# W' of three batches by Strassen's method in blocks, with the scores of later batches closer together

## The chip, the cores and the metric

The program runs on one core of a Trainium2 chip. The metric is the device time of one execution in microseconds (us), as a median of three runs. Of the core's engines, TensorE (PE in the profile) multiplies, VectorE (DVE) and ScalarE (ACT) do elementwise work, and SyncE (SP) issues the DMA transfers. Each engine works through its own list in order and waits where an operand or a buffer is not ready.

## The reference

```
B, N, C = 4, 6080, 256          d_model = 256, d_ff = 2048
qn = q / (norm(q, axis=1) + 1e-6);  kn = k / (norm(k, axis=1) + 1e-6)
a  = softmax(kn^T @ qn / tau, last axis) with + 1e-9 in the divisor     # 256 x 256 for each batch
x  = (v @ a) as 24320 rows of 256
out = max(0.01 h, h) @ w_out,  h = x @ w_in                            # float32 throughout
```

## The kernel before, in words

The kernel never forms x. Since h = v (a w_in), it makes W' = a w_in (256 x 2048) once for each batch and multiplies v by it. All products are in float32 precision from fp32r halves: each operand is split into a high and a low part, and three passes (high x high, low x high, high x low) are added up in PSUM.

**Tiles and steps.** The rows of v are taken in 24 tiles, six for each batch: five of 2 x 512 columns and one of 2 x 480. Each tile i is worked through in NPAIR = 8 steps p, each with one pair of blocks of W'; this text counts steps as s = 8 i + p, from 0 to 191, 48 for each batch. A step multiplies v by W' with Strassen's method in Winograd's form, seven products of three matmuls: A11 and A12 first, then S2, S1, S3, A22 and S4 (`block_product`), into the PSUM banks x and z. Between them ScalarE copies h11, h12 and h22 out of bank x (`taken`), VectorE adds bank z to them (`add`), and `leaky` applies the activation and splits the result. The step's 24 matmuls with w_out (`ffn_out`, L675) are issued during the next step by `out(n)`, in blocks of 5, 5, 8 and the remaining 6. So a step has 21 + 24 = 45 matmuls.

**Work beside it.** What the next batch needs is made during the current one: the scores k^T q of the 48 chunks (`chunk_work`: `cast` on ScalarE, `low` on VectorE, four matmuls `product`, and the squares for the norms), the norms and the softmax (`norm_work`, `row_work`), the transpose (`turn_work`) and then W' (`w_work`). The scores of batches 0 and 1 are made at the start of the program. W_in, split into halves, lies in DRAM as `win_dram` in blocks of 512 columns. A W' product (`w_product`, L463) has 6 matmuls: three passes over the two halves of the inner dimension; there are two for each of NWC = 4 column blocks j. Its copy goes to `w_parts`, which makes the sums of the blocks and splits them in six pieces: two sums (0.8 each), then `begin` (1.0) and `rest` (1.2) for each of two p. Every `begin` and `rest` takes a buffer of the tag qk_split (three buffers) and stores it to `w_dram`. The score casts use the same tag. `w_load` fetches the split blocks three steps ahead.

**The order.** The order on TensorE, VectorE and ScalarE is that of the program text: `in_order` ties each instruction to the one before it on its engine. DMA issues are not tied in that way. The work beside stands in queues `todo`, with a length for each entry that is a planner's figure; `slot(queue, room)` takes entries from the head as long as they fit. An entry may put others when it is issued, at the head where `first` is set. This text names the slots of a step (i > 0) in their order in the program:

- after A11 and A12: A1 (act, 0.65), the addition to h11, D1 (dve, 1.3), `out(5)`, P1 (pe, room 1)
- `leaky` of C11, D2 (dve, 2.2), block S2, the copy of h12, A2 (act, 1.8), block S1, `out(5)`, P2 (pe, 1)
- block S3, the copy of h22 and the addition to it, D3 (dve, 1.3), `out(8)`, P3 (pe_late, 1)
- `leaky` of C22, blocks A22 and S4, the addition to h12, `leaky` of C21, A3 (act, 0.65), D4 (dve, 0.8), `leaky` of C12, `out(24)`

The feed-forward work on v for the next tile (`v_work`) also stands in the dve queue. Work for batch b starts at `w0` = 48 (b - 1); `at(w, ...)` puts it at step w. Before, the norms come at step e, the rows at e + 2, the transpose at e + 4 and W' from e + 5 on.

Of the kernel before, what the change touches and what calls it, by code (L numbers as in the profile page):

```python
# [17 lines left out]
P = 128  # L18
TW = 512
# [5 lines left out]
WARM = 5  # L25
VBUFS = 10
# [6 lines left out]
def channel_attention_ffn(  # L33
# [44 lines left out]
    def temp(dtype=F32, name="temp"):  # L78
        return work.tile([P, TW], dtype, name=name, tag="temp", bufs=10)
# [34 lines left out]


    class Scores:
# [133 lines left out]
        def norms_begun(self):  # L250
# [84 lines left out]
        def turned_high(self):  # L335
            self.aT = small.tile([P, 2, CH, C], F32R, name="aT")
            return nc.scalar.copy(out=self.aT[:, 0], in_=self.t_ps)

        def turned_low(self):
            return nc.vector.tensor_tensor(  # L340
                out=self.aT[:, 1], in0=self.t_ps, in1=f32(self.aT[:, 0]), op=ALU.subtract
            )

# [93 lines left out]
    def win_load(j):  # L437
        for h in range(CH):
            win[j, h] = win_tile(False)
            nc.sync.dma_start(out=flat(win[j, h]), in_=win_dram[j][h])  # L440


# [25 lines left out]
    def w_tmp(name):  # L468
        return work.tile([P, TW], F32, name=name, tag="w_tmp", bufs=4)
# [81 lines left out]
    def w_load(i, p):  # L551
        w = w_tile()
# [107 lines left out]
    def ffn_out(i, p):  # L660
# [8 lines left out]
        for name, f, j in (("C11", f1, 0), ("C22", f2, 1), ("C21", f2, 0), ("C12", f1, 1)):  # L669
# [13 lines left out]
            if p == NPAIR - 1 and not early:  # L683
# [5 lines left out]
                for h, a, z, copy, queue in parts:  # L689
                    o = work.tile([P, TW], F32, name="o_sb", bufs=4)  # L690
# [21 lines left out]
    def put(queue, length, fn, then=(), first=False):  # L712
# [10 lines left out]

        (todo[queue].appendleft if first else todo[queue].append)((length, run))
# [8 lines left out]

    def chunk_work(sc, j):

        put("act", 0.6, lambda: sc.cast(j), [
            ("dve", 0.75, lambda: sc.low(j), [("pe_next", 1, lambda: sc.product(j))]),
        ])
# [400 lines left out]
```

## Time and profile before

| what | value |
|---|---|
| median of three runs | 2163.67 us (2163.30 to 2164.05) |
| the profiled execution | 2164.93 us, of which its span 2163.1 us |
| TensorE, matmuls | 2155.5 us busy, 9674 instructions |
| TensorE, weight loads | 1797.3 us busy |
| VectorE | 1464.7 us busy, 2602 instructions |
| ScalarE | 1468.1 us busy, 2545 instructions |
| DMA | 337.15 MB, 155 GB/s of HBM traffic over the span |

The span runs from the first to the last instruction. Matmuls overlap each other, so their busy time is that in which at least one runs. A share of busy time is an average over the whole span; what a change is worth is read from the place where it is made and from what waits there.

### The profile page before, as it was taken

The numbers are of one execution on the slowest core, as the hardware profiler recorded it, in microseconds if no ns is written. First come the engines' busy times: TensorE is split into PE (matmuls) and PEld (weight loads), VectorE is DVE, ScalarE is ACT, GpSimd is POOL, SyncE is SP. The second block draws the span as 40 slices with busy tenths as digits, with TensorE's granted clock in tenths as the row PEclk, the third lists the DMA queues.
The fourth block names the chain that finished last, engine by engine and source line by source line (L and its number), as shares of the span: only waits on it lengthen the run. The fifth ranks groups of instructions, "written<-read, shape, count | busy, mean of one in ns | idle before, by whom it ended". The sixth has DMA issues, their size and how long they took to land.

```text
span 2163.1 us, 26727 instructions
## 1 busy us (share of the span) xinstructions
PE 2155.5 (100%) x9674; PEld 1797.3 (83%) x9674; DVE 1464.7 (68%) x2602; ACT 1468.1 (68%) x2545; POOL 3.3 (0%) x11
## 2 busy tenths in 40 slices
PE   9999999999999999999999999999999999999999
PEld 8888888888888888888888888888888888888887
DVE  7987667657767666776776767666667555555554
ACT  6577777766677777776667777777656666666665
POOL 0000000000000000000000000000000000000000
PEclk9999999999999999999999999999999999999999
DMA  9945445435544343442654434344264332332331
GB/s 345 391 174 184 161 147 189 158 109 197 197 169 153 125 147 114 163 161 86 216 175 171 150 122 155 131 138 153 88 229 173 114 131 105 109 137 104 106 121 35
DMA packets 106179, 337.15 MB, mean 156 GB/s; under 512 B 11072, under 2 KB 23360, under 8 KB 106048
## 3 DMA queue, kind: packets, MB, share of 16 engines
q1 hardware_dynamic: 105680, 335.14, 44.9%
q8 instruction: 76, 1.25, 0.2%
q14 instruction: 55, 0.45, 0.1%
q10 hardware_dynamic: 368, 0.32, 0.1%
HBM read 276.96 MB, written 58.46 MB: 155 GB/s over the span
## 4 chain that ended last, share of the span: by engine, by line
PE 97%; DMA 1%; DVE 1%; ACT 0%; issue 0%; SPq 0%; ACTq 0%; DVEq 0%
PE ps_o L675 48%; PE ps_x L628 24%; PE ps_z L628 18%; PE ps_s L193 3%; PE ps_s L463 2%; PE ps_y L193 2%; PE ps_o L193 1%; DMA qk_raw<-in_k_dram 1%; PE ps_y L463 0%; PE ps_y L628 0%; DVE v_split L593 0%; SPq L141 0%; PE ps_z L463 0%; DVE h L649 0%; DVE g_split L642 0%
## 5 line engine op out<-in xcount | busy, mean ns | idle before, releaser
L675 PE MATMUL ps_o<-g_split,w_out_split 128*128 128x512 f32 (+1 forms) x4608 | 1161.6, 387 | 0.0
L675 PEld LDWEIGHTS ps_o<-g_split,w_out_split 128*128 128x128 f32 x4608 | 864.7, 188 | 173.9
L642 DVE TENSOR_TENSOR g_split<-h,g_split 128x512 fp32r<-128x512 f32 (+1 forms) x768 | 524.8, 684 | 387.7 <-ACT g_split L640 386.9
L628 PE MATMUL ps_x<-v_split,w_split 128*128 128x512 f32 (+1 forms) x2304 | 647.6, 389 | 0.0
L649 DVE TENSOR_TENSOR h<-ps_z,h 128x512 f32<-128x512 f32 (+1 forms) x568 | 387.4, 682 | 269.1 <-ACT h L655 263.7
L639 ACT ACTIVATE h<-h 128x512 f32<-128x512 f32 (+1 forms) x576 | 361.9, 628 | 263.1 <-DVE h L649 263.1
L655 ACT COPY h<-ps_x 128x512 f32<-128x512 f32 (+1 forms) x576 | 334.3, 580 | 297.5 <-PE ps_x L628 297.0
L628 PEld LDWEIGHTS ps_x<-v_split,w_split 128*128 128x128 f32 x2304 | 424.7, 188 | 80.3 <-ACT h L655 1.3
L640 ACT CAST g_split<-h 128x512 fp32r<-128x512 f32 (+1 forms) x768 | 473.6, 617 | 24.2
L628 PE MATMUL ps_z<-v_split,w_split 128*128 128x512 f32 (+1 forms) x1704 | 477.0, 388 | 0.3 <-DVE h L649 0.3
L628 PEld LDWEIGHTS ps_z<-v_split,w_split 128*128 128x128 f32 x1704 | 319.0, 188 | 66.8 <-DVE h L649 2.5
L639 ACT ACTIVATE h<-ps_x 128x512 f32<-128x512 f32 (+1 forms) x192 | 112.8, 588 | 11.6 <-PE ps_x L628 11.4
L593 DVE TENSOR_TENSOR v_split<-v_raw,v_split 128x512 fp32r<-128x512 f32 (+1 forms) x144 | 98.6, 686 | 5.8 <-DMA f_raw<-in_w_out_dram 0.6
L163 DVE TENSOR_TENSOR sq_acc<-sq_acc,sq 128x512 f32<-128x512 f32 x141 | 96.1, 682 | 0.0
L160 ACT ACTIVATE sq<-qk_raw 128x512 f32<-128x512 f32 x141 | 89.4, 634 | 0.0
L168 ACT CAST qk_split<-qk_raw 128x512 fp32r<-128x512 f32 x96 | 59.4, 619 | 25.5 <-PE ps_y L193 21.7
L172 DVE TENSOR_TENSOR qk_split<-qk_raw,qk_split 128x512 fp32r<-128x512 f32 x96 | 65.6, 683 | 2.3 <-ACT qk_split L168 2.3
L193 PE MATMUL ps_s<-qk_split 128*128 128x512 f32 x192 | 64.0, 333 | 0.0
L193 PE MATMUL ps_y<-qk_split 128*128 128x512 f32 x192 | 59.8, 336 | 0.0
L589 DVE CAST v_split<-v_raw 128x512 fp32r<-128x512 f32 (+1 forms) x138 | 57.3, 415 | 0.0
L193 PE MATMUL ps_s<-qk_raw 128*128 128x256 f32 x192 | 44.1, 381 | 1.8 <-DMA qk_raw<-in_k_dram 1.8
L193 PE MATMUL ps_o<-qk_raw 128*128 128x256 f32 x192 | 43.5, 390 | 0.4 <-DMA qk_raw<-in_k_dram 0.4
(113 smaller groups left out, 731.6 us busy)
## 6 DMA issues: line engine op xcount, KB each, us to landing
w_split<-w_dram SPq DMA_DIRECT2D x184, 896.0 KB, 4.7
qk_raw<-in_q_dram SPq DMA_DIRECT2D x115, 256.0 KB, 3.6
qk_raw<-in_k_dram SPq DMA_DIRECT2D x115, 256.0 KB, 4.1
v_raw<-in_vT_dram SPq DMA_DIRECT2D x40, 512.0 KB, 5.5
out_dram<-o_sb SPq DMA_DIRECT2D x80, 256.0 KB, 3.7
win<-win_dram SPq DMA_DIRECT2D x24, 512.0 KB, 3.9
w_dram<-w_rest SPq DMA_DIRECT2D x24, 512.0 KB, 3.1
w_dram<-w_first SPq DMA_DIRECT2D x24, 384.0 KB, 3.0
```

The lines of the kernel that those rows point to most:

```text
L160: return nc.scalar.activation(out=out, in_=self.chunk(j), func=AF.Square)
L163: return nc.vector.tensor_tensor(out=self.acc[0], in0=self.acc[0], in1=sq, op=ALU.add)
L172: return nc.vector.tensor_tensor(out=sp[:, :, 1, :], in0=self.chunk(j), in1=f32(sp[:, :, 0, :]), op=ALU.subtract)
L193: mm = nc.tensor.matmul(out=out, lhsT=lhsT, rhs=rhs, start=start, stop=stop, skip_group_check=True)
L593: last = nc.vector.tensor_tensor(out=sp[:, 1, 0:w], in0=src, in1=f32(sp[:, 0, 0:w]), op=ALU.subtract)
L628: mm = nc.tensor.matmul(out=ps[:, 0:n], lhsT=w[:, x, a, :], rhs=sp[:, y, 0:n], start=first and k == 0, stop=k == 2, skip_group_check=True,)
L639: nc.scalar.activation(out=out[:, 0:n], in_=h[:, 0:n], func=AF.Prelu, alpha=0.01)
L640: issued["act"] = nc.scalar.copy(out=sp[:, 0, 0:n], in_=out[:, 0:n])
L642: issued["dve"] = nc.vector.tensor_tensor(out=sp[:, 1, 0:n], in0=out[:, 0:n], in1=f32(sp[:, 0, 0:n]), op=ALU.subtract)
L649: issued["dve"] = nc.vector.tensor_tensor(out=h[:, 0:n], in0=ps[:, 0:n], in1=h[:, 0:n], op=ALU.add)
L655: issued["act"] = nc.scalar.copy(out=h[:, 0:n], in_=ps[:, 0:n])
L675: issued["pe"] = nc.tensor.matmul(out=o_ps[i][j][h][:, 0:n], lhsT=wo[x][:, f, h * P:(h + 1) * P], rhs=sp[:, y, 0:n], start=p == 0 and earl ...
```

## The change

W' of batches 1 to 3 is multiplied in blocks. With the four 128 x 128 blocks of a and the 128 x 512 blocks of W_in, two neighbouring column blocks (a pair q) take seven products of three matmuls, where they took four of six. `w_pair` issues them one after another: the first four add up in one PSUM bank and are copied by ScalarE after each, the last three are added by VectorE to those copies. After the seventh, `split(0)` and `split(1)` put the twelve pieces of `w_parts`, and the second pair follows. The sums of the W_in blocks are made once, at steps 10 and 20 (`sums_work`), and kept in DRAM as `win_sums`. The sums of the blocks of a and their halves are made after the transpose (`blocks_taken` to `blocks_low`). Of batch 0, W' stays as it was.

The chain from the norms to W' is now put as one list in which each entry follows when the one before it has been issued (`put_steps`), and cut finer: `norms_begun` has one Newton step, `norms_went` two; `maxima` is apart from `scaled`. The scores of batches 2 and 3 start at offset 0 of their 48 steps and take 28 instead of 31; the squares of batch 1 take 20 steps instead of 25. A cast waits in its queue while three are ahead of their products, and P1 takes up to three entries when at least two wait. Buffers: `temp` has 12 and serves `o_sb` too (before 10, and 4 of its own), `w_tmp` 6 instead of 4.

```
     def temp(dtype=F32, name="temp"):
-        return work.tile([P, TW], dtype, name=name, tag="temp", bufs=10)
+        return work.tile([P, TW], dtype, name=name, tag="temp", bufs=TEMPS)
...
             self.nt = small.tile([P, n], F32, name="nt")
-            return self.newton(x, self.ny, self.nt, 2)
+            return self.newton(x, self.ny, self.nt, 1)
+
+        def norms_went(self):
+            return self.newton(self.nx, self.ny, self.nt, 2)
 
         def norms(self):
             x, y, t, n = self.nx, self.ny, self.nt, 2 * CH
-            self.newton(x, y, t, 1)
...
-                nc.vector.scalar_tensor_tensor(
+                last = nc.vector.scalar_tensor_tensor(
                     out=s[:, h, :], in0=self.sum_of(h), scalar=self.rk[:, h:h + 1], in1=self.rq,
                     op0=ALU.mult, op1=ALU.mult,
                 )
+            self.e = s
+            return last
+
+        def maxima(self):
             self.nm = small.tile([P, CH], F32, name="nm")
-            self.e = s
-            return nc.vector.tensor_reduce(out=self.nm, in_=s, axis=AX.X, op=ALU.max, negate=True)
+            return nc.vector.tensor_reduce(out=self.nm, in_=self.e, axis=AX.X, op=ALU.max, negate=True)
...
     def w_tmp(name):
-        return work.tile([P, TW], F32, name=name, tag="w_tmp", bufs=4)
 
     def w_load(i, p):
+        assert (i // NT, p) in w_done
...
                 for h, a, z, copy, queue in parts:
-                    o = work.tile([P, TW], F32, name="o_sb", bufs=4)
+                    o = work.tile([P, TW], F32, name="o_sb", tag="temp", bufs=TEMPS)
                     copy(out=o[:, a:z], in_=o_ps[i][j][h][:, a:z])
                     queue.dma_start(out=outT[h * P:(h + 1) * P, n0 + a:n0 + z], in_=o[:, a:z])
...
-        while todo[queue] and todo[queue][0][0] <= room:
+        while todo[queue] and todo[queue][0][0] <= room and todo[queue][0][1].ready():
...
-        ])
+        def cast():
+            cast_ahead.append(j)
+            return sc.cast(j)
+
+        def product():
+            cast_ahead.pop(0)
+            return sc.product(j)
+
+        put("act", 0.6, cast, [("dve", 0.75, lambda: sc.low(j), [("pe_next", 1, product)])],
+            ready=lambda: len(cast_ahead) < 3)
...
     def norm_work(sc):
-        norms = ("pe_late", 1, sc.norms_mm, [
-            ("dve", 0.5, sc.norms_taken, [("dve", 1.8, sc.norms_begun, [("dve", 2.0, sc.norms)], True)], True),
-        ])
-        if len(sc.s) == 1:
-            put(*norms)
-        else:
-            put("act", 0.8, sc.cross_taken, [("dve", 0.9, sc.cross_added), norms])
-
-    def row_work(sc):
-        put("pe_late", 1, sc.rows_mm, [
-            ("dve", 0.5, sc.rows_taken, [
-                ("dve", 1.8, sc.scaled, [("act", 0.6, sc.exps, [("dve", 1.1, sc.normed, (), True)], True)], True),
-            ], True),
-        ])
+        norms = [("pe_late", 1, sc.norms_mm), ("dve", 0.4, sc.norms_taken), ("dve", 0.9, sc.norms_begun),
+                 ("dve", 1.2, sc.norms_went), ("dve", 1.2, sc.norms), ("pe_late", 1, sc.rows_mm),
+                 ("dve", 0.5, sc.rows_taken), ("dve", 1.0, sc.scaled), ("dve", 0.7, sc.maxima),
+                 ("act", 1.3, sc.exps), ("dve", 1.1, sc.normed), ("call", turn_work, sc)]
+        if len(sc.s) > 1:
+            norms[:0] = [("act", 0.8, sc.cross_taken), ("dve", 0.9, sc.cross_added)]
+        put_steps(norms, False)
 
     def turn_work(sc):
-        put("pe", 1, sc.turn, [("act", 0.6, sc.turned_high, [("dve", 0.7, sc.turned_low, (), True)], True)])
-
-    def w_work(b, j, h=0):
-
-
-        def taken():
-            ins = w_taken(b, j, h)
-            if h == 0:
-                w_work(b, j, 1)
+        put_steps([("pe", 1, sc.turn), ("act", 0.65, sc.blocks_taken), ("dve", 0.9, sc.blocks_summed),
+                   ("act", 1.3, sc.blocks_high), ("dve", 1.3, sc.blocks_low), ("call", w_pair, sc.b, 0)], False)
...
+    def sums_work(q):
+
+        blocks = {(h, x): win_in(win_dram[2 * q + x][h]) for h, x in ((0, 1), (0, 0))}
+        t = {}
...
+        def halves(name, x):
+            def high():
+                t[name, 0] = work.tile([P, 2, TW], F32R, name="win_t", tag="qk_split", bufs=3)
+                return nc.scalar.copy(out=t[name, 0][:, 0, :], in_=t[name])
+
+            def low():
+                r = t[name, 0]
+                ins = nc.vector.tensor_tensor(out=r[:, 1, :], in0=t[name], in1=f32(r[:, 0, :]), op=ALU.subtract)
+                nc.sync.dma_start(out=win_sums[q][x], in_=flat(r))
+                return ins
+            return [("act", 0.65, high), ("dve", 0.7, low)]
+
+        def more():
+            for h, x in ((1, 1), (1, 0)):
+                blocks[h, x] = win_in(win_dram[2 * q + x][h])
+
+        put_steps([
+            whole("a", 0, 1), whole("b", 0, 0), minus("b", "a", "b"), *halves("b", 0),
+            ("call", more),
+            whole("c", 1, 1), minus("a", "c", "a"), *halves("a", 2), minus("c", "c", "b"), *halves("c", 1),
+            whole("d", 1, 0), minus("d", "d", "c"), *halves("d", 3),
+        ], False)
+
+    A_S1, A_S2, A_S3, A_S4, A_11, A_12, A_22 = range(7)
+
+    def w_pair(b, q):
+
+        operands = [win_dram[2 * q][0], win_sums[q][1], win_sums[q][2], win_sums[q][3],
+                    win_sums[q][0], win_dram[2 * q + 1][1], win_dram[2 * q][1]]
+        of = (A_11, A_S2, A_S3, A_22, A_S1, A_S4, A_12)
+        loaded, c = {}, {}
+
+        def load(n):
+            if n < 7:
+                loaded[n] = win_in(operands[n])
+
+        def product(n):
+            m, r = scores[b].m, loaded.pop(n)
+            if n in (0, 4, 6):
+                c["ps"] = bank("s")
+            for k, (x, y) in enumerate(PASSES):
+                last = nc.tensor.matmul(
+                    out=c["ps"], lhsT=m[:, x, of[n], :], rhs=r[:, y, :], start=n in (0, 4, 6) and k == 0, stop=k == 2,
+                    skip_group_check=True,
+                )
+            load(n + 2)
+            return last
+
+        def taken(n):
+            if n == 0:
+                for name in ("c11", "c21", "c12", "c22"):
+                    c[name] = w_tmp("w_a")
+            out = c[("c11", "c12", "c22", "c21", "c22", "c12", "c11")[n]]
+            if n < 4:
+                return nc.scalar.copy(out=out, in_=c["ps"])
+            return nc.vector.tensor_tensor(out=out, in0=out, in1=c["ps"], op=ALU.add)
+
+        def split(x):
+            j = 2 * q + x
+            for h in range(CH):
+                a_sb[b, j, h] = c[("c11", "c21", "c12", "c22")[2 * x + h]]
+            for length, fn in w_parts(b, j):
+                put("dve", length, fn)
+            length, fn = todo["dve"].pop()
+            if x == 0:
+                put("dve", length, fn, [("call", split, 1)])
+            elif q + 1 < NWC // 2:
+                put("dve", length, fn, [("call", w_pair, b, q + 1)])
             else:
-                for length, fn in w_parts(b, j):
-                    put("dve", length, fn)
-                if j + 1 < NWC:
-                    length, fn = todo["dve"].pop()
-                    put("dve", length, fn, [("call", w_work, b, j + 1)])
-            return ins
-
-        if h == 0 and j + 1 < NWC:
-            win_load(j + 1)
-        put("pe", 1, lambda: w_product(b, j, h, "s"), [("act", 0.6, taken, (), True)])
+                todo["dve"].append((length, fn))
+
+        def step(n):
+            after = [("call", step, n + 1)] if n < 6 else [("call", split, 0)]
+            put("pe", 1, lambda: product(n), [
+                ("act" if n < 4 else "dve", 0.65, lambda: taken(n), after, True)
+            ])
+
+        load(0)
+        load(1)
+        step(0)
...
     for b in range(1, B):
         w0 = (b - 1) * WPB
         sc = scores[b]
-        begin_at, span = (NPAIR, 25) if b == 1 else (2, 31)
+        begin_at, span = (NPAIR, 20) if b == 1 else (0, 28)
         when = {j: w0 + begin_at + j * span // NCHUNK for j in range(NCHUNK)}
         for i in range(len(sc.groups)):
-            at(max(w0, when[i * G] - 3), lambda sc=sc, i=i: sc.load(i, qk_raw()))
+            at(max(w0 - 2, when[i * G] - (1 if b == 1 else 3)), lambda sc=sc, i=i: sc.load(i, qk_raw()))
         for j in range(NCHUNK):
             at(when[j], square_work if b == 1 else chunk_work, sc, j)
         e = w0 + begin_at + span + 1
         at(e, norm_work, sc)
-        at(e + 2, row_work, sc)
-        at(e + 4, turn_work, sc)
-        at(e + 1, win_load, 0)
-        at(e + 5, w_work, b, 0)
+    for pair in range(NWC // 2):
+        at(10 + 10 * pair, sums_work, pair)
...
             out(5)
-            slot("pe", 1 if i else 2)
+            slot("pe", 1 if i and len(todo["pe"]) < 2 else 3)
```

## Rows read from the trace of the kernel before

**Rows 1.** The profile page of the kernel before: busy time of TensorE (PE) and of its weight loads (PEld) with their shares of the span and their instructions, and TensorE's granted clock in 40 slices, in tenths of full speed.

```profile
PE 2155.5 (100%) x9674; PEld 1797.3 (83%) x9674; DVE 1464.7 (68%) x2602; ACT 1468.1 (68%) x2545; POOL 3.3 (0%) x11
...
PEclk9999999999999999999999999999999999999999
```

**Rows 2.** The page's chain of work that ended last: shares of the span by engine.

```profile
PE 97%; DMA 1%; DVE 1%; ACT 0%; issue 0%; SPq 0%; ACTq 0%; DVEq 0%
```

**Rows 3.** The same chain in order of time: start in us, length in us, engine, tile, line and count of the merged piece. Each row is the third output block of a step (8 matmuls of L675), of which every step has one: steps 9 and 10, which hold no other matmuls, two neighbours in the scores of batch 2, and two neighbours in the stretch in which W' of batch 2 is made.

```profile
197.62 1.81 PE ps_o L675 x8
...
207.82 1.81 PE ps_o L675 x8
...
637.35 1.82 PE ps_o L675 x8
...
648.97 1.82 PE ps_o L675 x8
...
1029.56 1.81 PE ps_o L675 x8
...
1042.48 1.81 PE ps_o L675 x8
```

**Rows 4.** Busy time in a stretch of ten steps of tile 2 and 3 (batch 1 squares running beside the feed-forward work): from, to, length, then busy us and instructions of PE, PEld, VectorE (DVE), ScalarE (ACT) and GpSimd, the granted clock, the DMA share and GB/s.

```profile
306.00:408.00 102.00, 102.00 (x451) 84.46 (x450) 71.96 (x116) 75.69 (x131) 0.00 (x0) 1.00 0.46 158
```

**Rows 5.** The instructions of L463, the W' products, in bank s (batches 1 to 3): shortest, median and longest duration in ns, first and last start, form.

```profile
L463 PEld LDWEIGHTS ps_s<-win,aT x144: 187/188/188, 502.2 to 1642.5; 128*128 128x128 f32 x144
L463 PE MATMUL ps_s<-win,aT x144: 387/393/398, 502.5 to 1642.7; 128*128 128x512 f32 x144
```

**Rows 6.** TensorE's instructions in order of time (start us, length us, engine, line, operation, output<-inputs, shape, count): around the norms and the exps of batch 2, the second W' product of step 87, and the A22 block of step 96.

```profile
986.21 1.98 PE L675 MATMUL ps_o<-g_split,w_out_split 128*128 128x512 f32 x8
988.20 1.02 PE L229 MATMUL ps_s<-ones,sq_acc 128*128 128x1 f32 x8
...
1007.79 1.98 PE L675 MATMUL ps_o<-g_split,w_out_split 128*128 128x512 f32 x8
1009.62 0.61 PE L284 MATMUL ps_y<-diag,ones 128*128 128x128 f32 x4
...
1018.47 1.98 PE L675 MATMUL ps_o<-g_split,w_out_split 128*128 128x512 f32 x8
1020.33 0.96 PE L628 MATMUL ps_x<-v_split,w_split 128*128 128x512 f32 x3
1021.13 0.87 PE L628 MATMUL ps_z<-v_split,w_split 128*128 128x512 f32 x3
...
1040.28 1.52 PE L463 MATMUL ps_s<-win,aT 128*128 128x512 f32 x6
...
1140.84 0.84 PE L628 MATMUL ps_x<-v_split,w_split 128*128 128x512 f32 x3
```

**Rows 7.** ScalarE's instructions in order of time, same columns; in brackets the idle time before one and what ended it. The copy of h22 behind the exps, the copy of a W' product, the copy of h22 in step 96, a score cast and the square behind it in step 98.

```profile
1019.72 0.56 ACT L655 COPY h<-ps_x 128x512 f32<-128x512 f32 x1
...
1039.14 0.59 ACT L473 COPY w_a<-ps_s 128x512 f32<-128x512 f32 x1
...
1139.29 0.59 ACT L655 COPY h<-ps_x 128x512 f32<-128x512 f32 x1 [1.68 <-PE ps_x L628]
...
1158.45 0.61 ACT L168 CAST qk_split<-qk_raw 128x512 fp32r<-128x512 f32 x1
1158.96 0.64 ACT L160 ACTIVATE sq<-qk_raw 128x512 f32<-128x512 f32 x1
```

**Rows 8.** VectorE's instructions in order of time, same columns: the first operation of the step in which the scores' halves are added, norms in batch 2, and in step 96 a rest, the start of the begin behind it, and an addition of 128x512.

```profile
987.63 0.41 DVE L208 TENSOR_TENSOR s_cross<-ps_s,s_cross 128x256 f32<-128x256 f32 x1
...
1006.99 0.16 DVE L266 TENSOR_TENSOR nt<-nx,ny 128x4 f32<-128x4 f32 x1
...
1007.74 0.47 DVE L276 TENSOR_SCALAR diag<-ident,rn 128x128 f32<-128x128 f32 x2
...
1135.72 0.49 DVE L508 CAST w_rest<-w_s 128x256 fp32r<-128x256 f32 x2
1136.12 0.75 DVE L509 TENSOR_TENSOR w_rest<-w_s,w_rest 128x256 fp32r<-128x256 f32 x2
...
1137.77 0.42 DVE L508 CAST w_first<-w_a 128x128 fp32r<-128x128 f32 x2
...
1139.91 0.69 DVE L649 TENSOR_TENSOR h<-ps_z,h 128x512 f32<-128x512 f32 x1
```

**Rows 9.** SyncE's queue in order of time: the load of the first chunk of batch 3, and the store of the rest of the rows above.

```profile
1086.66 0.53 SPq L136 DMA_DIRECT2D qk_raw<-in_q_dram  x1
...
1136.90 0.52 SPq L524 DMA_DIRECT2D w_dram<-w_rest  x1
```

**Rows 10.** Who waited for whom: engine, line, releaser: us in total, times, longest us.

```profile
ACT qk_split L168 <- PE ps_y L193: 21.7, 16, 1.9
```

**Rows 11.** The stores of W' pieces (L524), from issue to landing.

```profile
DMA to landing us min/median/max: 2.8/3.1/6.8
```

**Rows 12.** The page's DMA issues: W_in blocks read back, KB each, median us from issue to landing.

```profile
win<-win_dram SPq DMA_DIRECT2D x24, 512.0 KB, 3.9
```

More of the change, by code (lines that the diff above doesn't have):

```diff
@@ L25 @@
 WARM = 5
+TEMPS = 12
 VBUFS = 10
@@ L342, in turned_low, with blocks_taken, blocks_summed, blocks @@
             )
+        def blocks_taken(self):
+            self.a = w_tmp("w_a")
+            return nc.scalar.copy(out=self.a, in_=self.t_ps.rearrange("p d c -> p (d c)"))
+        def blocks_summed(self):
+            self.a_s = w_tmp("w_s")
+            a11, a21, a12, a22 = (self.a[:, x * P:(x + 1) * P] for x in range(4))
+            s1, s2, s3, s4 = (self.a_s[:, x * P:(x + 1) * P] for x in range(4))
+            for out, x, y, op in ((s1, a21, a22, ALU.add), (s3, a11, a21, ALU.subtract),
+                                  (s2, s1, a11, ALU.subtract), (s4, a12, s2, ALU.subtract)):
+                last = nc.vector.tensor_tensor(out=out, in0=x, in1=y, op=op)
+            return last
+        def blocks(self):
+            flat = self.m.rearrange("p x s c -> p x (s c)")
+            for src, at in ((self.a_s, 0), (self.a[:, 0:P], 4 * P), (self.a[:, 2 * P:4 * P], 5 * P)):
+                n = src.shape[1]
+                yield src, flat[:, 0, at:at + n], flat[:, 1, at:at + n]
+        def blocks_high(self):
+            self.m = m_tile()
+            for src, hi, _ in self.blocks():
+                last = nc.scalar.copy(out=hi, in_=src)
+            return last
+        def blocks_low(self):
+            for src, hi, lo in self.blocks():
+                last = nc.vector.tensor_tensor(out=lo, in0=src, in1=f32(hi), op=ALU.subtract)
+            return last
     def f64_load(bits):
@@ L435, in win_block @@
         return w_in[h * P:(h + 1) * P, j * TW:(j + 1) * TW], halves, store
[L437 to L440, printed above, removed]
     w_split = {}
@@ L468, in w_tmp @@
     def w_tmp(name):
-        return work.tile([P, TW], F32, name=name, tag="w_tmp", bufs=4)
+        return work.tile([P, TW], F32, name=name, tag="w_tmp", bufs=6)
     def w_taken(b, j, h):
@@ L710, in slot, with put @@
             issued[engine] = ins
-    def put(queue, length, fn, then=(), first=False):
+    def put(queue, length, fn, then=(), first=False, ready=lambda: True):
         def run():
@@ L722, in run @@
             return ins
+        run.ready = ready
         (todo[queue].appendleft if first else todo[queue].append)((length, run))
@@ L732, in acc_tile @@
         return work.tile([P, 2, C], F32, name="sq_acc", bufs=1)
+    cast_ahead = []
     def chunk_work(sc, j):
-        put("act", 0.6, lambda: sc.cast(j), [
-            ("dve", 0.75, lambda: sc.low(j), [("pe_next", 1, lambda: sc.product(j))]),
-        ])
+        def cast():
[6 more added lines that the diff above has]
+            ready=lambda: len(cast_ahead) < 3)
         if j == 0:
@@ new lines, in win_in, with whole, fn, minus @@
+    def win_in(src):
+        r = win_tile(False)
+        nc.sync.dma_start(out=flat(r), in_=src)
+        return r
+    def sums_work(q):
+        blocks = {(h, x): win_in(win_dram[2 * q + x][h]) for h, x in ((0, 1), (0, 0))}
+        t = {}
+        def whole(name, h, x):
+            def fn():
+                r = blocks[h, x]
+                t[name] = w_tmp("win_s")
+                return nc.vector.tensor_tensor(out=t[name], in0=f32(r[:, 0, :]), in1=f32(r[:, 1, :]), op=ALU.add)
+            return ("dve", 0.7, fn)
+        def minus(out, x, y):
+            return ("dve", 0.7, lambda: nc.vector.tensor_tensor(out=t[out], in0=t[x], in1=t[y], op=ALU.subtract))
+        def halves(name, x):
[17 more added lines that the diff above has]
+        ], False)
@@ L808, in entry @@
         def entry(n):
-            return (*steps[n], [entry(n + 1)] if n + 1 < len(steps) else (), first or n > 0)
+            then = [entry(n + 1)] if n + 1 < len(steps) else ()
+            if steps[n][0] == "call":
+                return ("call", lambda: (steps[n][1](*steps[n][2:]), *(put(*x) for x in then)))
+            return (*steps[n], then, first or n > 0)
         put(*entry(0))
@@ L955, in channel_attention_ffn @@
     run("dve", sc.norms_begun)
+    run("dve", sc.norms_went)
     run("dve", sc.norms)
@@ L965, in channel_attention_ffn @@
     run("dve", sc.scaled)
+    run("dve", sc.maxima)
     conv_begin()
```

6 lines of the change are left out of this document (5 added, 1 removed).

## Prediction, made before the changed kernel ran

> **What bounds the kernel now.** The profile page comes first. [...] The chain of waits, read next, stays on TensorE for 97% [rows 2]; merged in order of time it gives the engine's pace. From the start of one step's third output block to that of the next, a step with nothing but its own 45 matmuls takes 10.20 us, that is 0.2267 us each; a step that also holds two products of W' (12 matmuls) takes 12.92 us, which is 2.72 us more and again 0.2267 each; one that holds two score products takes 1.42 us more [rows 3]. Nothing is lost between them, so a matmul taken out gives back 0.2267 us, and a wait of TensorE costs its full length. Everything on VectorE, ScalarE and the queues is free up to the moment at which it makes TensorE wait. A plain stretch leaves VectorE 30 and ScalarE 26 of 102 us [rows 4].
>
> [...]
>
> **Part 1: the products.** Before, a batch has 8 products of 6 matmuls of 512 columns, 48, or 144 for three batches [rows 5]. After, each of two pairs of blocks has 7 products of 3 passes: 42. Three batches lose 18 matmuls: 18 x 0.2267 = 4.1 us less. This is certain, and all that the change can gain by itself is 0.19%; about 0.2% (4.3 us) is what a measurement of this kernel can tell from nothing.
>
> **Part 2: sums, splits and copies.** The sums of W_in cost 24 VectorE operations of about 0.69 us (the 128x512 rows of [rows 8]) and 8 casts of about 0.61, some 16 and 5 us, in steps 10 to 13 and 20 to 23. Four steps there last 41 us, in which VectorE has 12 us free after [rows 4] and needs 8 more, plus a quarter more squares: it fits. In three of those steps a cast waits for the second subtraction of its step, and the copy of h22 stands behind it on ScalarE. The same shape is in the rows: the exps end so late that the copy of h22 starts at 1019.72 [rows 7], and the next block runs at 1020.33 instead of 1.82 us after 1018.47 and its successor late too, together about 0.15 us [rows 6]. That is 3 x 0.15 lost. The exps themselves now come a slot earlier in each of three batches, because the scaling has moved ahead of the maxima: 3 x 0.15 won. I cancel the two, with 0.5 us either way.
>
> The scores are closer (28 steps in place of 31) but have the same matmuls, and a product costs 0.71 us wherever it stands. Casts already wait for their buffers, 16 times and 21.7 us [rows 10], at no cost to TensorE in the score steps; the new limit of three casts ahead takes such waits away. Nothing here, to within 0.5 us.
>
> **Part 3: the chain of norms.** It ran with fixed distances; now each operation follows as soon as a slot takes it. Played through with the lengths of the code, batches 1 to 3 do the same, in steps 30, 78 and 126: norms_begun (0.9) takes D1, norms_went (1.2) takes D2 and leaves no room for norms (1.2), which takes D3; the very next place in the order is P3, where rows_mm needs its result. In the rows D3 begins 1.42 us after the out(8) block (987.63 against 986.21 [rows 6, 8]). What is left of norms, from L266 to the second diag, takes 1.22 us (1006.99 to 1007.74 plus 0.47) [rows 8]. A matmul starts about 0.16 us behind the VectorE operation it waits for (988.20 after 987.63 plus 0.41). So the second rows_mm starts 2.80 us after the block, while P3 comes 1.83 us after it (1009.62 against 1007.79) [rows 6]: up to 0.97 us of waiting, and 0.74 if it is the first diag that counts. Below: nothing, if norms found a place in D2. I take 0.85, three times: 2.6 us. Behind the waiting rows_mm stand this step's A22 and S4 blocks and all that follows.
>
> **Part 4: W' tail against the scores' start.** The score work of a batch now begins at offset 0 instead of 2, in the step in which the last pieces of the batch before it are still split. Played through, steps 48 and 96 hold, in this order: the first cast (A1), a `begin` (D1), a `rest` and a `begin` (D2), square, second cast, square (A2), then ScalarE's copy of h22, a `rest` (D3). Casts and pieces all take buffers of qk_split, of which there are three, and a piece gives its buffer back only when its store has landed. The first cast holds its buffer until the product in the next step. The two others go to the first `begin` and `rest`; the second `begin` takes the first to come back, and the second cast has to wait for the store of that `rest`.
>
> Step 96 of before supplies the times. D2 starts at 1137.77; a `rest` takes 1.15 us (1135.72 to 1136.87) [rows 8], its store is issued 0.03 later [rows 9] and lands after 3.1 us [rows 11]: 1137.77 + 1.15 + 0.03 + 3.1 = 1142.05. The waiting cast and square follow each other by 0.51 us, so the copy of h22 runs from 1143.07 for 0.59 us instead of from 1139.29 [rows 7]. A22, which overwrites what that copy reads, goes at about 1143.7 instead of 1140.84 [rows 6]: 2.9 us on TensorE, twice: 5.8 us. If the cast is given the first buffer instead, `begin` waits on VectorE, the addition behind it makes S4 late, and it is about 2.0 us each. Below: nothing, if both were free in time; above: a store that lands in 6.8 us [rows 11] makes it 6.6 each. I take 2.9, since the store is the median one.
>
> **Sum.** -4.08 + 2.55 + 5.8 = +4.27. The profiled execution took 2164.93 us, its span 2163.1 and 1.8 around it, which does not change; it stands 1.26 us above the median of 2163.67. Span 2167.4, profiled 2169.2, median 2167.9.
>
> **Rivals.**
> Only the norms wait (15%): the pieces' stores come back in time. Then -4.08 + 2.55 = -1.5: 2162.2. For it speaks that casts wait elsewhere without harm [rows 10]; against it that those waits are at most 1.9 us.
>
> Neither wait (11%): -4.1, or -4.6 with the exps' gain and no cost of the sums: 2159.3, just at the edge of being told from no change. It needs a D2 with room for norms.
>
> The second pair's first load is late (9%). In the code it stands behind the last `rest` and its store. If SyncE takes them in that order, 512 KB land 3.9 us after issue [rows 12], behind 1.15 us of `rest`, where the product is due at once: 5 us, three times, 2167.9 + 15 = 2183. It decides from the point at which the load is issued less than 4 us ahead. Against it: the load of batch 3's first chunk, which the code places in step 96 (the one whose A22 is at 1140.84), was issued at 1086.66 [rows 6, 9], as soon as a buffer was free.
>
> One bank hands over too late (6%). Seven products now pass through one PSUM bank, each waiting for a copy or an addition of the one before. Two products in one step have 0.55 us to spare (the copy ends 1039.14 plus 0.59, the next product starts 1040.28 [rows 6, 7]), and there are 18 such pairs of neighbours. Slipping by two instructions of 0.65 us would cost 18 x 0.75 = 13.5 us: 2181. Against it: before has the same hand-over in every W' step and loses nothing [rows 3]. [...]
>
> A longer store (7%): it lands after 5 us, between the median and the longest [rows 11], and each collision costs 4.8 instead of 2.9: 2171.7. Two more stores and the casts' loads share the queues in those steps.
>
> **How the numbers follow.** The forecast has 52%, its own range 2165.5 to 2170.5 (2.0 to 3.3 us at each collision, 0.5 to 0.97 at each norms). The bound for faster is 2159.3, for slower 2168.0, and the forecast lies just inside it: half of its chance counts as slower. Slower is then 0.26 with the late load, the bank and the longer store, 0.48; faster half of "neither wait", 0.06; no change the rest, 0.46. I move 0.04 from slower to faster for gains in the queues that I do not see. From 2159.3 to 2173 the late load, the bank and half of "neither wait" stay outside, 2 in 10.
>
> **What would show it.** The profile after should count 126 matmuls of the products (42 a batch); hold waits of rows_mm of about 0.9 us at the three norms; a cast waiting some 4 us in ScalarE's list at the start of batches 2 and 3, with a gap of 2.9 us ahead of A22; no wait ahead of a pair's first product. The forecast fails if the queues fill otherwise than I played them, if buffers come back earlier than the store's landing, or if the sums delay VectorE by more than its room.

## The result, and the profile after

The changed kernel takes 2175.8 us, the median of six runs (2174.27 to 2176.25), the kernel before 2163.58 beside it: a ratio of 1.0055 with a 95% interval of 1.0044 to 1.0066. It is 12.2 us slower. The forecast was 2167.9 us, and 2173.0 the upper end of its range, so direction and place were right and the size was not. The profiled execution took 2174.88 us, its span 2173.0: 9.9 us above the span of before. The other 2.3 us between the medians are that the profiled execution of before stood 1.3 us above its median and that of after 0.9 below. Three executions far outside all others (2690, 6276 and 12473 us, among the runs of the experiments) stand in no comparison below.

The page of after: busy time by engine, the granted clock in 40 slices, the chain's shares by engine. They answer to [rows 1, 2].

```profile
PE 2156.5 (99%) x9656; PEld 1793.2 (83%) x9656; DVE 1492.9 (69%) x2662; ACT 1473.5 (68%) x2562; POOL 3.3 (0%) x11
...
PEclk9999999999999999999999999999999999999999
...
PE 91%; DVE 4%; ACT 3%; DMA 1%; issue 1%; SPq 0%; ACTq 0%; DVEq 0%
```

TensorE has 18 matmuls fewer and is busy for 1 us longer. The chain has left it for another 6% of the span, in favour of VectorE and ScalarE. The 40 slices still show a full clock: a fall of a few microseconds can't be seen in slices of 54 us. The mean granted clock of this execution is 0.998.

**The products** are as forecast. TensorE in order of time in the W' stretch of after, out(8) of two neighbouring steps and the two products between them:

```profile
458.30 1.98 PE L711 MATMUL ps_o<-g_split,w_out_split 128*128 128x512 f32 x8
...
465.32 0.84 PE L874 MATMUL ps_s<-win,aT 128*128 128x512 f32 x3
...
468.50 0.84 PE L874 MATMUL ps_s<-win,aT 128*128 128x512 f32 x3
469.86 1.98 PE L711 MATMUL ps_o<-g_split,w_out_split 128*128 128x512 f32 x8
```

Such a step lasts 11.56 us, 1.36 more than a plain one for two products, where two of the old ones took 2.72 [rows 3]. Fourteen times 0.68 against eight times 1.36, three batches: -4.08 us. No product waited for the one bank or for a load: the trace has no idle time of TensorE ahead of any of the 126 matmuls of L874.

**The norms** lose what was forecast. TensorE again, out(8) around the rows_mm of batch 1, then the group of waits of all three batches (total, times, longest):

```profile
415.68 1.98 PE L711 MATMUL ps_o<-g_split,w_out_split 128*128 128x512 f32 x8
...
427.20 1.98 PE L711 MATMUL ps_o<-g_split,w_out_split 128*128 128x512 f32 x8
```

```profile
PE ps_y L290 <- DVE diag L282: 1.7, 3, 0.6
```

11.52 us, where the step with rows_mm took 10.68 before (1007.79 to 1018.47 [rows 6]). The three steps are 0.85, 0.80 and 0.79 us longer, 2.4 in all; the matmuls' own wait explains 0.62, 0.53 and 0.53 of it. The rest, 0.23 to 0.27 us, is what a step loses beyond its wait, which this text calls the refill: the weight loads ahead of the waiting matmuls stood idle for 1.01, 0.95 and 0.95 us, and in batch 1 the first block behind the wait took 0.78 us to the start of the next (418.72 to 419.50), where a block in TensorE's pace takes 0.68.

**Step 48** shows the collision. ScalarE, VectorE, SyncE and TensorE of after, each in order of time (in brackets the idle time before, and what ended it); last, TensorE's granted clock by stretches, the first figure behind the last bracket of a row:

```profile
610.80 0.62 ACT L172 CAST qk_split<-qk_raw 128x512 fp32r<-128x512 f32 x1 [4.02 <-DMA w_dram<-w_rest]
611.32 0.62 ACT L164 ACTIVATE sq<-qk_raw 128x512 f32<-128x512 f32 x1
611.85 0.57 ACT L691 COPY h<-ps_x 128x512 f32<-128x512 f32 x1
```

```profile
609.14 0.43 DVE L543 CAST w_first<-w_a 128x128 fp32r<-128x128 f32 x2 [1.58 <-DMA w_dram<-w_first]
```

```profile
607.59 0.52 SPq L559 DMA_DIRECT2D w_dram<-w_rest  x1
```

```profile
607.74 1.90 PE L711 MATMUL ps_o<-g_split,w_out_split 128*128 128x480 f32 x8
612.47 1.65 PE L664 MATMUL ps_x<-v_split,w_split 128*128 128x512 f32 x3 [2.83 <-ACT h L691]
613.92 1.48 PE L664 MATMUL ps_z<-v_split,w_split 128*128 128x512 f32 x3
615.20 1.65 PE L711 MATMUL ps_o<-g_split,w_out_split 128*128 128x480 f32 x6
616.69 0.86 PE L664 MATMUL ps_x<-v_split,w_split 128*128 128x512 f32 x3
...
623.28 2.01 PE L711 MATMUL ps_o<-g_split,w_out_split 128*128 128x512 f32 x8
```

```profile
610.00:612.00 2.00, 0.00 (x0) 0.00 (x0) 0.11 (x1) 1.20 (x3) 0.00 (x0) 1.00 0.42 154
612.00:613.00 1.00, 0.53 (x1) 0.51 (x2) 0.55 (x1) 0.42 (x1) 0.00 (x0) 0.58 0.40 141
613.00:614.00 1.00, 1.00 (x4) 0.74 (x3) 1.00 (x5) 0.79 (x2) 0.00 (x0) 0.50 0.00 0
614.00:615.00 1.00, 1.00 (x4) 0.80 (x3) 1.00 (x3) 1.00 (x3) 0.00 (x0) 0.50 0.00 0
615.00:616.00 1.00, 1.00 (x4) 0.81 (x4) 0.94 (x2) 0.41 (x1) 0.00 (x0) 0.72 0.00 0
616.00:617.00 1.00, 1.00 (x6) 0.83 (x5) 0.24 (x2) 0.77 (x2) 0.00 (x0) 1.00 0.74 100
```

This is Part 4 step by step: the store of the `rest` issued at 607.59, the second cast held for 4.02 us until it has landed, its square and the copy of h22 behind it, and A22 after 2.83 us of waiting (forecast: some 4, and 2.9). Step 96 has the same with 3.98 and 2.80:

```profile
1148.41 0.62 ACT L172 CAST qk_split<-qk_raw 128x512 fp32r<-128x512 f32 x1 [3.98 <-DVE w_first L544]
```

Here the profile names VectorE's `begin`, but that ended at 1147.94; the store of the `rest`, issued at 1145.24, lands at 1148.35, and the cast starts 3.2 us behind the issue in both steps. What the forecast lacks is the price of the wait. From 612.2 to 615.6 the granted clock is at 0.50. The next three blocks, 12 matmuls from A22 on, take 4.22 us (612.47 to 616.69); with the clock at 1.00 they took 2.84 in the third experiment. In step 48 it falls 0.3 us before TensorE resumes, in step 96 1.4 us after it (low from 1151.5 to 1154.9, TensorE from 1150.09).

Where the scores start later, the steps 48 and 96 cost 10.25 and 10.27 us (first and last experiment), and 0.71 more with the one score product that they hold here: 10.96 and 10.98. They last 15.54 us and 15.68: 9.3 us too long together, forecast 5.8.

**The sums** are the second loss. ScalarE in step 23 of after, where high casts of the sums of W_in stand in L836, and TensorE's out(8) around the steps 23 and 24:

```profile
341.55 0.62 ACT L836 CAST win_t<-win_s 128x512 fp32r<-128x512 f32 x1 [1.60 <-DVE win_s L831]
342.07 0.63 ACT L164 ACTIVATE sq<-qk_raw 128x512 f32<-128x512 f32 x1
342.61 0.57 ACT L691 COPY h<-ps_x 128x512 f32<-128x512 f32 x1
```

```profile
341.35 1.98 PE L711 MATMUL ps_o<-g_split,w_out_split 128*128 128x512 f32 x8
...
352.89 2.00 PE L711 MATMUL ps_o<-g_split,w_out_split 128*128 128x512 f32 x8
...
363.72 1.99 PE L711 MATMUL ps_o<-g_split,w_out_split 128*128 128x512 f32 x8
```

Steps 23 and 24 last 11.54 and 10.83 us instead of 10.20, steps 11 and 12 10.60 and 11.25: 3.4 us in all. In four of the eight casts ScalarE waits for VectorE's subtraction (5.7 us in all), with the feed-forward's copy behind the cast: 1.60 us in steps 11, 12 and 23, and 0.88 in step 20, which lost nothing.

Small rests: the step with the exps lasts 10.69 us, before 10.93 (-0.7 in three batches); the start is 0.7 us shorter, no gain to count on (the first out(8) starts at 102.62 here and at 104.07 in the first experiment, whose edit does not touch the start); a step at a tile boundary (16) is 0.3 longer. The sum is -4.1 + 2.4 + 9.3 + 3.4 - 0.7 - 0.7 + 0.3 = 9.9 us, the difference of the spans.

### The profile page after: what moved, and what is told of

It reads as the page before. It is cut to its first block, busy times and chain, and to the rows that moved or that the text cites. A ratio compares the mean times of both kernels' runs of the same rounds, so it can differ in the third digit from the quotient of the medians.

```text
span 2173.0 us, 26914 instructions
## 1 busy us (share of the span) xinstructions
PE 2156.5 (99%) x9656; PEld 1793.2 (83%) x9656; DVE 1492.9 (69%) x2662; ACT 1473.5 (68%) x2562; POOL 3.3 (0%) x11
## 4 chain that ended last, share of the span: by engine, by line
PE 91%; DVE 4%; ACT 3%; DMA 1%; issue 1%; SPq 0%; ACTq 0%; DVEq 0%
PE ps_o L711 44%; PE ps_x L664 22%; PE ps_z L664 17%; PE ps_s L197 3%; PE ps_y L197 2%; PE ps_s L874 1%; DVE h L685 1%; PE ps_o L197 1%; DVE g_split L678 1%; DMA qk_raw<-in_k_dram 1%; ACT g_split L676 1%; ACT h L675 1%; ACT h L691 0%; PE ps_y L498 0%; DVE v_split L629 0%
## 5 line engine op out<-in xcount | busy, mean ns | idle before, releaser
L675 ACT ACTIVATE h<-h 128x512 f32<-128x512 f32 (+1 forms) x576 | 361.9, 628 | 303.2 <-DVE h L685 303.2
L675 ACT ACTIVATE h<-ps_x 128x512 f32<-128x512 f32 (+1 forms) x192 | 113.1, 589 | 13.5 <-PE ps_x L664 13.2
```

The source lines that it names most:

```text
L675: nc.scalar.activation(out=out[:, 0:n], in_=h[:, 0:n], func=AF.Prelu, alpha=0.01)
```

## The experiments

The theory: three faults of timing outweigh the products, namely the early scores (wait and clock), the norms' wait and the sums' casts; each can be removed alone, and they add. The rivals: one of them is not the cause, or the loss moves elsewhere. All edits are against the changed kernel, unless said otherwise.

**The scores one step later.**

```
-        begin_at, span = (NPAIR, 20) if b == 1 else (0, 28)
+        begin_at, span = (NPAIR, 20) if b == 1 else (1, 27)
```

> The changed kernel with the scores of batches 2 and 3 from offset 1 in 27 steps (ending where they ended), so that no score cast stands in steps 48 and 96 beside the last W' pieces. Theory (the casts wait for qk_split buffers, ScalarE's copy of h22 waits behind them, TensorE waits 2.8 us and its granted clock then falls): both gaps of 2.8 us and both stretches at the lower clock go, the mean granted clock is 1.000, and the time falls by 2 x 4.7 = 9.4 us, from 2175.8 to about 2166.4. Rival (the clock falls because the stretch around batch starts has less matmul work in it, or the wait only moves into step 49): a gap or a low clock stays near the start of each batch and less than 5 us come back.

2166.01 us (2164.64 to 2166.90), ratio to before 1.0011 (1.0002 to 1.0019). TensorE's out(8) at the two ends of step 48:

```profile
609.13 1.90 PE L711 MATMUL ps_o<-g_split,w_out_split 128*128 128x480 f32 x8
...
619.38 1.98 PE L711 MATMUL ps_o<-g_split,w_out_split 128*128 128x512 f32 x8
```

Nothing is lost in step 48 any more (10.25 us), and the mean granted clock is 1.000 in all eleven runs. The collision cost 9.8 us by the medians and 9.3 by the steps, the clock included.

**Only the second chunk later.**

```
+        if b > 1:
+            when[1] = w0 + 1
```

> The changed kernel with one entry moved for each of batches 2 and 3: the second score chunk starts in step 49 or 97 instead of 48 or 96. The first cast still holds a buffer and the second begin still waits for a store on VectorE (1.6 us in the trace), but no cast stands ahead of the copy of h22. Theory: A22 goes on time, S4 is late by about 0.5 us, the clock stays up: about 2 x 4.2 = 8.4 us come back, 2167.4. Rival (any wait for a buffer in that step is enough, on VectorE too): S4 waits 1.5 us or more and at most 5 us come back in all, 2170.8 or more.

2167.94 us (2167.17 to 2169.82), ratio 1.002 (1.0011 to 1.0028). The clock stays at 1.00, and the steps 48 and 96 are still 11.80 and 12.24 us long, 0.8 and 1.3 too long: 0.54 and 0.96 us of waiting for VectorE's addition and the refill behind it. 7.9 us came back where 8.4 were expected. So one cast alone in the step is not free either.

**The norms asked for in D2.**

```
-                 ("dve", 1.2, sc.norms_went), ("dve", 1.2, sc.norms), ("pe_late", 1, sc.rows_mm),
+                 ("dve", 1.2, sc.norms_went), ("dve", 1.0, sc.norms), ("pe_late", 1, sc.rows_mm),
```

> The changed kernel with the planner's length of norms set to 1.0 instead of 1.2, which lets it into D2 behind norms_went, one slot ahead of D3. Nothing else is moved. Theory: rows_mm finds its result ready in steps 30, 78 and 126, the three waits of 0.8 us go, and 2.4 us come back: 2173.4. Rival (VectorE is late as a whole there, so that the addition to h22 and S4 pay for it): the wait moves to A22 or S4 and the time stays within 0.8 us of 2175.8.

2171.82 us (2170.61 to 2174.84), ratio 1.0039 (1.0026 to 1.0052): 4.0 less where 2.4 were expected. The three steps are back at 10.67, the whole 2.4. In the profiled execution (2170.61 us, the fastest of the five) more is seen in step 48, which this edit does not touch; TensorE there, then its clock by stretches:

```profile
612.88 0.96 PE L664 MATMUL ps_x<-v_split,w_split 128*128 128x512 f32 x3 [3.04 <-ACT h L691]
...
615.72 0.85 PE L664 MATMUL ps_x<-v_split,w_split 128*128 128x512 f32 x3
```

```profile
610.00:612.00 2.00, 0.00 (x0) 0.00 (x0) 0.61 (x3) 0.79 (x2) 0.00 (x0) 1.00 0.27 98
612.00:614.00 2.00, 1.11 (x5) 0.82 (x6) 1.14 (x4) 1.24 (x3) 0.00 (x0) 1.00 0.46 166
614.00:616.00 2.00, 2.00 (x11) 1.70 (x10) 2.00 (x5) 1.97 (x5) 0.00 (x0) 1.00 0.08 30
```

The wait is as long as in the changed kernel, and the clock did not fall. The steps 48 and 96 are then 3.4 and 3.1 us too long instead of 4.6 and 4.7. So the waits themselves cost 6.4 us, and the lower clock 2.8 where it comes in both places. This does not explain the median: in the other four runs the mean granted clock is 0.997 or 0.998, as low as in the changed kernel, and yet the median is 4.0 us less. Where the clock stays up, the same edit gives 2.6 us (2166.01 to 2163.44, the first experiment against the eighth). The other 1.4 us of the median's 4.0 stay open.

**The sums' high casts on VectorE.**

```
-                return nc.scalar.copy(out=t[name, 0][:, 0, :], in_=t[name])
+                return nc.vector.tensor_copy(out=t[name, 0][:, 0, :], in_=t[name])
...
-            return [("act", 0.65, high), ("dve", 0.7, low)]
+            return [("dve", 0.42, high), ("dve", 0.7, low)]
```

> The changed kernel with the high halves of the W_in sums (8 casts of 128x512) written by VectorE in the dve queue instead of by ScalarE, so that no cast on ScalarE waits for a subtraction ahead of a copy of h12 or h22. Theory: the lost 3.4 us of steps 11, 12, 23 and 24 come back, 2172.4, and the 8 casts (about 0.42 us each on VectorE) are hidden. Rival (VectorE has too little room there, with sums, squares and v beside each other): those steps stay 0.5 us or more over 10.20 us, and at most 1 us comes back.

2176.01 us (2174.90 to 2178.35), ratio 1.0059 (1.0046 to 1.0073): as a total a miss. ScalarE's waits for the sums are gone and the steps 11 and 12 last 10.20 us each. But the second pair's last cast came 11 us after its subtraction (346.16, behind 335.08), held up by the work on v, and the steps 23 to 25 lost 4.0 us. ScalarE there; the changed kernel waits 0.6 us for an output store at this place:

```profile
361.81 0.63 ACT L164 ACTIVATE sq<-qk_raw 128x512 f32<-128x512 f32 x1 [2.98 <-DMA out_dram<-o_sb]
```

The squares that the sums had held up come at once behind the tile boundary and run round the 12 buffers of temp into one that `o_sb` holds until the output's store has landed. The cause of the first place was right, and the repair made a second collision of the same kind. The clock fell in step 96 of this execution but not in step 48 (mean 0.999, as in four of the five runs), so the total is without some of what the clock costs the changed kernel.

**The same, and the second pair's sums from step 18 on.**

```
-        at(10 + 10 * pair, sums_work, pair)
+        at(10 + 8 * pair, sums_work, pair)
```

> The changed kernel with the sums of W_in repaired in both places: the high casts of the sums (after's line 836) go from ScalarE to VectorE, 0.42 us each, and the second pair's sums begin at step 18 instead of step 20, so that none of them lies in steps 23 to 25 around a tile boundary. Theory: the changed kernel lost 3.4 us in steps 11, 12, 23 and 24 because ScalarE, in order, waited 1.60 us for VectorE in four of the eight casts (5.7 us in all); the same casts on VectorE at step 20 freed steps 11 and 12 and lost 4.0 us around step 24, where the last block's sums met the work on V (VectorE idle 3.5 us, ScalarE 3.0 us behind a store of the output). At step 18 both are gone: steps 11 to 25 at 10.20 us, about 2172.4 us. Rival: the sums cost VectorE's time wherever they stand, another three steps are longer and the time stays at 2175.8 us.

2171.47 us (median of five, 2168.38 to 2173.43), ratio 1.0034 (1.0022 to 1.0046), -4.3 where -3.4 were expected. TensorE's out(8) at the two ends of step 23:

```profile
340.82 1.98 PE L711 MATMUL ps_o<-g_split,w_out_split 128*128 128x512 f32 x8
...
351.02 1.98 PE L711 MATMUL ps_o<-g_split,w_out_split 128*128 128x512 f32 x8
```

10.20 us, and so are the steps 11, 12 and 24 but for 0.35 at the boundary and 0.24 more in step 18. Steps 10 to 25 are 2.8 us shorter than in the changed kernel. The rest of the 4.3 need not be the sums': the mean granted clock of the median run is 0.999, that of the changed kernel's 0.998, and the profiled execution, in which it is 0.998 too, takes 2172.54 us. So the sums do fit into VectorE's room, if ScalarE needs not wait for them and they end ahead of the boundary.

**A fourth buffer of qk_split** (all five lines of the tag), with `TEMPS` 10 instead of 12 to make room.

```
-TEMPS = 12
+TEMPS = 10
...
-            sp = work.tile([P, 2, 2, C], F32R, name="qk_split", bufs=3)
+            sp = work.tile([P, 2, 2, C], F32R, name="qk_split", bufs=4)
```

> The changed kernel with four buffers of qk_split instead of three; to make room, temp has 10 buffers instead of 12. Scores, norms and sums as in the changed kernel. Theory: in steps 48 and 96 the second cast waits for a buffer that a rest holds until its store has landed (issued at 607.59, the cast starts at 610.80). With a fourth buffer the second begin needs not wait, and the cast takes the buffer of the first begin, whose store landed at 609.14 in the changed kernel: the cast starts some 1.7 us earlier, TensorE's two waits of 2.8 us shrink to about 1.1 us, and the granted clock stays at 1.00 there: 2175.8 - 2 x (1.7 + 1.4) = 2169.6 us. Ten buffers of temp can cost a little at the tile boundaries. Rival: the cast waits for something else that ends then (its input, the queue); then a buffer more changes nothing: 2175.8 us.

2176.97 us (2176.46 to 2177.40), ratio 1.0063 (1.005 to 1.0076): no gain in the total, and yet the buffer is the cause. TensorE in step 48, then ScalarE, in step 48 and at the tile boundary of step 24:

```profile
618.75 0.96 PE L664 MATMUL ps_x<-v_split,w_split 128*128 128x512 f32 x3 [1.44 <-ACT h L691]
```

```profile
617.08 0.62 ACT L172 CAST qk_split<-qk_raw 128x512 fp32r<-128x512 f32 x1 [2.63 <-DMA w_dram<-w_first]
```

```profile
364.79 0.59 ACT L691 COPY h<-ps_x 128x512 f32<-128x512 f32 x1 [5.40 <-DMA out_dram<-o_sb]
```

The cast now waits for a `begin`'s store instead of a `rest`'s, TensorE 1.44 and 1.57 us instead of 2.83 and 2.80, the clock stays at 1.00 there, and the steps 48 and 96 are each 2.8 us shorter. With ten buffers of temp a copy out of bank x waits 5.40 us for the output's store; TensorE stands for 4.95, and the clock falls 1.1 us before it resumes (low from 364.3 to 371.1). Step 24 lasts 18.14 us, 7.3 more than in the changed kernel, and gives back more than the 5.6 that the two others gained.

**The early scores in the kernel before**, an edit of before, which has no Strassen products in W' and no sums.

```
-        begin_at, span = (NPAIR, 25) if b == 1 else (2, 31)
+        begin_at, span = (NPAIR, 25) if b == 1 else (0, 33)
```

> The kernel before with one edit: the later batches' scores begin in the first step of the previous batch, (0, 33) for (2, 31); it has neither Strassen's products nor sums. Theory: the loss of steps 48 and 96 is that the first chunk's three casts need a buffer of qk_split that the pieces of W' hold until their stores have landed; it needs only the early start, so the kernel before must show it too: TensorE idle 2.5 to 3.0 us in both steps behind ScalarE, 5.0 to 6.0 us if the granted clock stays at 1.00 and about 9 if it falls as in the changed kernel: 2168.6 to 2172.6 us. Rival: the early start harms only where W' ends later, behind Strassen's products: no gap, 2163.6 us.

2172.24 us (2171.81 to 2173.18), ratio 1.0037 (1.0024 to 1.0051). TensorE in steps 48 and 96, and two stretches of clock behind each wait:

```profile
610.34 0.97 PE L628 MATMUL ps_x<-v_split,w_split 128*128 128x512 f32 x3 [3.10 <-ACT h L655]
...
1147.52 1.07 PE L628 MATMUL ps_x<-v_split,w_split 128*128 128x512 f32 x3 [3.01 <-ACT h L655]
```

```profile
610.00:612.00 2.00, 1.66 (x7) 1.29 (x8) 1.29 (x2) 1.21 (x3) 0.00 (x0) 1.00 1.01 373
612.00:614.00 2.00, 2.00 (x11) 1.66 (x10) 1.64 (x3) 1.76 (x4) 0.00 (x0) 1.00 0.47 134
```

```profile
1149.00:1150.00 1.00, 1.00 (x4) 0.81 (x3) 0.46 (x1) 1.00 (x2) 0.00 (x0) 0.50 0.00 0
1150.00:1151.00 1.00, 1.00 (x4) 0.79 (x4) 1.00 (x3) 0.76 (x2) 0.00 (x0) 0.50 0.20 43
```

This one edit of the kernel before makes 8.5 us, where the changed kernel lost 12.2. The rival falls: the collision needs neither Strassen's products nor a later end of W'.

**Scores and norms together.** The edits of the first and the third experiment.

> The changed kernel with the later batches' scores a step later and closer, (1, 27) for (0, 28), and the norms asked for in the slot D2 (1.0 for 1.2). Theory: the terms add. The scores gave 9.8 us, the norms' three waits are 0.85, 0.80 and 0.79 us, 2.4 us: 2175.8 - 9.8 - 2.4 = 2163.6 us, the time of the kernel before; the sums' 3.4 us remain and eat most of what the products save. Rival: the norms gave 4.0 us by themselves, so the waits cost more than the three steps show: 2162.0 us.

2163.44 us (2162.48 to 2164.04), ratio 0.9998 (0.9989 to 1.0007): the terms add, to the time of before.

**All three.** Scores (1, 27), norms in D2, the sums' casts on VectorE and the second pair's from step 18.

> All three repairs together: scores (1, 27), norms in D2, the sums' high casts on VectorE and the second pair's sums from step 18. Theory: 2175.8 - 9.8 - 2.4 - 3.4 = 2160.2 us, about 3.4 us below the kernel before, which is the products' 4.1 us and the closer exponentials' 0.7 us less what small rests remain. Rival: the sums' loss only moves (2163.6 us).

2160.49 us (2160.17 to 2161.62), ratio 0.9985 (0.9976 to 0.9994). The one group left in which TensorE waits for a copy of the feed-forward, at the start of the program:

```profile
PE ps_x L664 <- ACT h L691: 0.7, 1, 0.7
```

This version beats both, if by little: 3.3 us below the kernel before, beside which it ran. Of the 4.1 us of the products and the 0.7 of the exps, 0.8 are lost again in the steps 16, 18 and 24.

## Why the prediction was right or wrong

- **What bounds the kernel: right.** Nearly all that was lost or won is a wait, a matmul or the lower clock of TensorE; with the start, the sum of the steps gives the span's 9.9 us. The 18 matmuls were worth 4.08 us, 0.2267 each.
- **Part 1, products: right** (-4.08), and with it the rivals of the one bank and of the late load: no wait ahead of L874. Seven products through one bank lost nothing: each copy or addition ended 0.48 us or more before the next product started.
- **Part 3, norms: right**, 0.85, 0.80, 0.79 for 0.85. One planner's figure, 1.2 for 1.0, was the whole of it.
- **Part 4, place and wait: right; price: wrong.** The cast's wait (4.02 for some 4), TensorE's (2.83 for 2.9) and their cause stand as told. The failed term is "2.9 us on TensorE, twice", and the step that failed is the premise that "a wait of TensorE costs its full length". A wait of 2.7 to 3.0 us cost 3.2 with the refill behind it where the clock stayed up (6.4 for the two, forecast 5.8), and 4.6 where the clock fell (9.3).
- **Part 2, sums: wrong in size.** The step that failed is "3 x 0.15 lost". The shape was seen (a cast that waits for the subtraction, the copy behind it), but its length was taken from the exps' row. Three casts did wait in the way, 1.60 us each (a fourth waited 0.88 without harm), but they cost their steps 0.4, 1.05 and 1.3 us; with 0.6 in step 24, at the tile boundary, of which 0.35 stays in the fifth experiment, that is 3.4 us. "It fits" was judged by VectorE's free time in a sum, which holds (the fifth experiment), but not by where in the step the pieces come.
- **The exps and the closer scores: right** within 0.5 us (-0.7 for -0.45, nothing).
- **The range** had a longer store (4.8 us at each collision, 7%: 2171.7), which comes near the 9.3 by luck: the store landed 3.0 to 3.1 us after its issue, as forecast. For what follows a wait it had nothing. The measured span is 5.6 us above the forecast one (2173.0 and 2167.4): 2.8 the clock, 0.65 the refill, 2.95 the sums, less 0.75 of small rests. The medians stand 2.3 us further apart, since the two profiled executions lay on different sides of theirs.

TensorE's wait came back at the same place of two batches, 2.83 and 2.80 us, and shrank to 1.44 and 1.57 with one buffer more: there the buffers were too few.

## What to carry to other kernels

A buffer that is freed only when its store has landed blocks an engine in order, and everything behind the blocked instruction (here ScalarE for 4.02 us, and TensorE behind it for 2.83); so look at who shares a buffer tag before moving work next to it, and move it by one step before adding buffers. Price a wait of the bounding engine at more than its length: waits of about 3 us cost here 0.2 to 0.6 us more where the clock stayed up, and 1.5 to 1.9 more where it fell. Free time of an engine in a stretch doesn't show that an operation on another engine can wait for it there (three casts waited 1.60 us each here).

## What the runs showed of the hardware

The granted clock fell from 1.00 to 0.50 at some waits of TensorE and not at others of the same length. It fell at 2.83 and 2.80 us (the changed kernel), 2.72 (step 96 of the fourth experiment), 3.07 and 2.78 (the fifth), 3.01 (step 96 of the kernel before with early scores) and 4.95 (four buffers). It stayed at 1.00 at 3.10 (step 48 of the kernel before with early scores), 3.04 and 2.73 (norms in D2), 2.83 (step 48 of the fourth experiment), and at 1.44 and 1.57. Two executions have both outcomes; here are the waits and the clock of the fourth experiment's:

```profile
613.77 0.96 PE L664 MATMUL ps_x<-v_split,w_split 128*128 128x512 f32 x3 [2.83 <-ACT h L691]
...
1150.14 0.96 PE L664 MATMUL ps_x<-v_split,w_split 128*128 128x512 f32 x3 [2.72 <-ACT h L691]
```

```profile
612.00:618.00 6.00, 4.22 (x17) 3.14 (x18) 4.21 (x10) 5.11 (x10) 0.00 (x0) 1.00 0.43 116
1151.70:1155.00 3.30, 3.30 (x10) 2.72 (x9) 3.03 (x7) 3.25 (x7) 0.00 (x0) 0.50 0.64 126
```

Once at 0.50, it stayed there for some 3.4 us (612.2 to 615.6 and 1151.5 to 1154.9 in the changed kernel), and for 6.8 at the wait of 4.95 (364.3 to 371.1), though TensorE was working again. The steps 48 and 96 of the runs with both early casts and three buffers are too long (their score products taken off) by 3.1 to 3.4 us where the clock stayed up and by 4.5 to 4.7 where it fell, whatever the order of the two in an execution; so the lower clock cost some 1.1 to 1.7 us each time. It fell before TensorE resumed (0.3 us in step 48 of the changed kernel) or after (1.4 us in step 96). What decides whether it falls these runs do not settle.
